# Lending the SBUF of resting weights to the K and V tiles between two layers of a decode kernel

## The chip, the cores and the metric

The kernel runs on one core of a Trainium2 chip. The metric is the device time in microseconds (us). The profiled span, which the profile counts its times from, is some 2 to 3 us shorter than the time. The time of one kernel varies by about 1% from run to run, so single runs are not compared where the difference is small. PE is TensorE, the engine of the matmuls. SyncE (SP in the profile) issues the loads here. PE's granted clock is the share of its full clock that the profile's clock records show.

## The reference

Two identical layers, each an attention block and a gated block, both with a layer norm and a residual. One new token per sequence, four sequences:

```python
B, Sq, D = 4, 1, 512
Hq, Hkv, Sk, Dh = 32, 8, 4096, 128        # four query heads share one K/V head
# attention: q = norm(x) @ wq; softmax(q k^T / sqrt(Dh)) v; @ wo
# gated block: h = sigmoid(norm(x) @ w_gate) * (norm(x) @ w_up); h @ w_down
x = x + A(norm(x)); x = x + B(norm(x))    # layer 1
x = x + A(norm(x)); x = x + B(norm(x))    # layer 2, same weights, same cache
```

Both layers read the same cache: 8 K/V heads ("groups") × 4 sequences × 2 (K and V) tiles of 1 MiB. That is 64 tiles per layer, and almost all of the traffic.

## The kernel before

K and V tiles pass through a ring of eleven SBUF tiles. The weights have fixed places and are loaded once. The second layer visits the groups in reverse, so that the last group of layer 1 (eight tiles) serves as the first of layer 2 without a load. The parts that matter here, with cuts:

```python
NS = 11
ring = [sb(f"ring{i}", [P, T * DH], bf) for i in range(NS)]
wq = sb("wq", [P, KD, H * DH], bf)
wu = sb("wu", [P, KD, F], bf)
wd = sb("wd", [P, 4, 3, D], bf)
wd_r = sb("wd_r", [P, 2, D], bf)
...
def pump():                       # loads, in the fixed order of the queue
    while queue:
        if isinstance(queue[0], tuple):
            if not free:
                return            # a K/V load needs a free tile
            load_kv(*queue.pop(0))
        else:
            queue.pop(0)()        # a weight has its own place

def done_with(n, kind):           # after group n's scores ("k") or values ("v")
    for b in range(B):
        if n == G - 1:
            slots[n + 1, kind, b] = slots[n, kind, b]   # shared by both layers
        else:
            free.append(slots[n, kind, b])
    pump()
```

All loads are issued by SyncE on one queue, in this order. Each waits on the semaphores of whatever last used its tile. In the last two groups of a layer the work is arranged for latency. In layer 2, three of the last group's V tiles go through one set of matmuls (`values(n + 1, (0, 1, 2))`), and the fourth has a path of its own, called "the last tile" here.

## Time and profile before

| | before |
|---|---|
| time, median of 3 | 382.67 us (382.48 to 382.71) |
| profiled span | 380.5 us |
| bytes read | 139.73 MB |
| loads stand still between the layers | about 215 to 225.5 us |
| last V tile landed (issue + time to landing: 355.1 + 11.5) | 366.6 us |
| its matmuls start | 369.18 us |
| w_down's matmuls of layer 2 start | 376.79 us |

These are two rows of the page: the span in 40 slices, with the busy share of the load engines in tenths and the rate they reached.

```profile
DMA  7999999999999999999999539999999999999940
GB/s 307 403 387 400 396 381 413 388 405 405 380 416 387 391 407 390 421 419 371 370 396 397 234 92 375 416 393 411 399 404 404 398 411 391 418 421 387 387 149 2
```

The loads run at about 400 GB/s everywhere except in the first slice, in slices 22 and 23 (counted from 0) and in the last two. So the time is the time of the loads plus two stretches without them. The table by windows shows the first stretch closely. Its columns are the stretch, its length, PE's granted clock, the share of the load engines and GB/s.

```profile
214.00:216.00 2.00, 1.00 0.30 127
216.00:218.00 2.00, 1.00 0.00 0
...
224.00:226.00 2.00, 0.97 0.51 66
226.00:228.00 2.00, 0.88 0.76 311
228.00:230.00 2.00, 0.50 0.88 326
```

Counting every window from 214 to 232 us against 400 GB/s (a window of 2 us at rate r loses 2 × (1 − r/400) us) gives 12.0 us of lost transfer time. The cause is in SyncE's timeline (start, length, what it issued, how many) and in its waits (who waited for whom, total us, times, longest us):

```profile
197.43 27.45 SPq L251 DMA_DIRECT2D ring<-in_A_k_cache_dram  x4
224.92 9.55 SPq L251 DMA_DIRECT2D ring<-in_A_v_cache_dram  x4
```

```profile
SPq L78 <- PE S_ps L437: 48.1, 9, 23.6
```

Four K loads in one row last 27 us because the fourth waited 23.6 us for layer 2's first scores (PE S_ps), the first event that freed a ring tile. Eight tiles were held by the shared group, and three had already been filled again.

The second stretch is the tail. This is PE's timeline there: the values matmuls of three V tiles, the last tile's matmuls (L567), then w_gate's and w_up's (L616), and w_down's (L658). A row gives start, length, line, what was done and how often; a bracket at its end gives the idle time before it and what ended that.

```profile
364.08 3.56 PE L513 MATMUL O_ps<-ring,pt_sb 128*16 128x512 bf16 x24 [2.35 <-issue]
...
369.18 0.62 PE L567 MATMUL S_ps<-ring,pt_sb 128*16 128x128 bf16 x32
...
374.26 0.93 PE L616 MATMUL O_ps<-wu,xT 128*4 128x448 bf16 x16
...
376.79 0.84 PE L658 MATMUL Y_ps<-wd,hT 128*4 128x128 bf16 x48
```

From the last tile's matmuls it takes 5.1 us until w_up is used and 7.6 us until w_down is used. During that time the load engines have nothing to do.

### The profile page before, as it was taken

To read this page: it belongs to the slowest core of one execution; us is meant where nothing else is said; L and a number is where in the kernel's file an instruction comes from. 1 tells how busy PE (TensorE), PEld (TensorE's weight loads), DVE (VectorE), ACT (ScalarE), POOL (GpSimd) and SP (SyncE) were. 2 spreads that over 40 slices of the span, in tenths; PEclk is the share of its full clock that TensorE was granted. 3 is DMA by queue.
4 is the path that set the end of the run, shared out by engine and by line. 5 is a ranking of instruction groups with operands and counts; after the bars stand their busy time and mean duration, and the time that the engine had idled before them with its cause. 6 is when DMAs were issued, how large, how long until landed. Compare 5 with 4: busy or idle time off the path is not lost. (4 is left out here: it accounts for less than half of the span.)

```text
span 380.5 us, 5087 instructions
## 1 busy us (share of the span) xinstructions
PE 179.4 (47%) x2136; PEld 77.6 (20%) x2136; DVE 195.3 (51%) x280; ACT 85.3 (22%) x169; POOL 9.8 (3%) x36
## 2 busy tenths in 40 slices
PE   0336243442454414522359856463444454541876
PEld 0213021121121211211124422121121121211333
DVE  3744733638355383398310348482928384697212
ACT  1113040040220402204210132323232231304311
POOL 6100000000000000000000000000000000000000
PEclk9995565555555555556669976665656566665589
DMA  7999999999999999999999539999999999999940
GB/s 307 403 387 400 396 381 413 388 405 405 380 416 387 391 407 390 421 419 371 370 396 397 234 92 375 416 393 411 399 404 404 398 411 391 418 421 387 387 149 2
DMA packets 48550, 140.06 MB, mean 368 GB/s; under 512 B 2192, under 2 KB 6544, under 8 KB 40848
## 3 DMA queue, kind: packets, MB, share of 16 engines
q1 hardware_dynamic: 48480, 139.73, 95.5%
q8 instruction: 17, 0.28, 0.3%
q14 instruction: 5, 0.04, 0.0%
q10 hardware_dynamic: 48, 0.01, 0.0%
HBM read 139.73 MB, written 0.00 MB: 367 GB/s over the span
## 5 line engine op out<-in xcount | busy, mean ns | idle before, releaser
L428 DVE STREAM_TRANSPOSE ring<-ring 128x2048 int32<-128x2048 int32 x60 | 137.2, 2299 | 40.8 <-DMA ring<-in_A_k_cache_dram 40.0
L454 ACT ACTIVATE p_sb<-S_ps,nbias,rs_q 128x1024 bf16<-128x1024 f32 x16 | 41.9, 2617 | 188.1 <-DVE nbias L450 188.1
L437 PE MATMUL S_ps<-ring,qbd 128*16 128x512 bf16 x512 | 56.5, 616 | 36.7 <-DVE ring L428 36.4
L513 PE MATMUL O_ps<-ring,pt_sb 128*16 128x512 bf16 x496 | 58.2, 605 | 10.9 <-DMA ring<-in_A_v_cache_dram 8.3
L447 DVE TENSOR_REDUCE ml<-S_ps 128x1 f32<-128x1024 f32 x16 | 19.5, 1219 | 51.5 <-PE S_ps L437 51.5
L466 PE MATMUL PT_ps<-sel_p,p_sb 128*128 128x64 bf16 x128 | 9.3, 235 | 62.5 <-ACT p_sb L454 62.5
L589 PE MATMUL Y_ps<-wo,oT 128*4 128x128 bf16 x256 | 7.9, 260 | 51.1 <-DVE oT L540 51.0
L437 PEld LDWEIGHTS S_ps<-ring,qbd 128*16 128x16 bf16 x512 | 15.7, 120 | 67.7 <-issue 42.4
L513 PEld LDWEIGHTS O_ps<-ring,pt_sb 128*16 128x16 bf16 x496 | 17.6, 122 | 40.7 <-issue 37.4
L524 ACT ACTIVATE o_sb<-O_ps,wcol 128x512 f32<-128x512 f32 x16 | 11.0, 687 | 54.3 <-PE O_ps L513 47.9
L466 PEld LDWEIGHTS PT_ps<-sel_p,p_sb 128*128 128x128 bf16 x128 | 7.0, 123 | 75.3 <-ACT p_sb L454 74.4
L476 DVE STREAM_TRANSPOSE tr<-ml 128x64 f32<-128x64 f32 x16 | 3.8, 237 | 28.9 <-ACT p_sb L454 28.9
L531 PE MATMUL M_ps<-ident,o_sb 128*128 128x128 f32 x64 | 13.3, 342 | 10.5 <-ACT o_sb L524 10.5
L589 PEld LDWEIGHTS Y_ps<-wo,oT 128*4 128x4 bf16 x256 | 4.1, 93 | 56.1 <-DVE oT L540 56.1
L416 ACT ACTIVATE qbd<-Q_ps 32x64 bf16<-32x64 f32 x60 | 12.9, 214 | 6.4 <-PE Q_ps L402 5.9
L336 PE MATMUL S_ps<-perm 128*128 128x256 bf16 x78 | 14.1, 288 | 0.0
L531 PEld LDWEIGHTS M_ps<-ident,o_sb 128*128 128x128 f32 x64 | 8.5, 169 | 21.5 <-ACT o_sb L524 20.5
L491 DVE TENSOR_TENSOR el<-ee,tr 128x16 f32<-128x16 f32 x16 | 2.8, 175 | 19.4 <-ACT ee L489 19.4
L471 ACT ACTIVATE pt_sb<-PT_ps 128x512 bf16<-128x512 f32 x16 | 9.5, 596 | 10.6 <-PE PT_ps L466 10.6
L402 PE MATMUL Q_ps<-qT,perm 128*128 128x16 bf16 x64 | 4.4, 179 | 15.7 <-ACT qT L399 15.5
L540 DVE TENSOR_REDUCE oT<-M_ps 128x16 bf16<-128x64 f32 (+1 forms) x16 | 3.1, 197 | 15.5 <-PE M_ps L531 15.5
L381 POOL TENSOR_TENSOR rs_h<-vpe,mhalf 128x1 f32<-128x1 f32 x2 | 1.1, 550 | 353.5 <-DVE vpe L377 200.5
(91 smaller groups left out, 111.5 us busy)
## 6 DMA issues: line engine op xcount, KB each, us to landing
ring<-in_A_k_cache_dram SPq DMA_DIRECT2D x60, 1024.0 KB, 14.1
ring<-in_A_v_cache_dram SPq DMA_DIRECT2D x60, 1024.0 KB, 17.2
wq<-in_A_wq_dram SPq DMA_DIRECT2D x4, 1024.0 KB, 14.2
wo<-in_A_wo_dram SPq DMA_DIRECT2D x4, 1024.0 KB, 14.6
wg<-in_B_w_gate_dram SPq DMA_DIRECT2D x1, 1792.0 KB, 16.3
wu<-in_B_w_up_dram SPq DMA_DIRECT2D x1, 1792.0 KB, 16.8
wd<-in_B_w_down_dram SPq DMA_DIRECT2D x1, 1536.0 KB, 23.7
wd_r<-in_B_w_down_dram SPq DMA_DIRECT2D x2, 128.0 KB, 21.0
```

Of the source, the lines that this page charges most:

```text
L336: fn = lambda e: e.matmul(bank[:, 0:256], lhsT=perm[:, 0, :], rhs=perm[:, 0:2, :].rearrange("p n x -> p (n x)"), start=True, stop=True)
L416: fns.append(lambda e, o=o, i=i: e.activation(o, i, ACTF.Copy))
L428: S.put("dve", lambda e: e.transpose(v, v), reads=[f"r{s}"], writes=[f"r{s}"])
L437: fns.append(lambda e, q=q, nn=nn, b=b, kt=kt: e.matmul(S_ps[32 * b:32 * b + 16, q * 512:(q + 1) * 512], lhsT=qbd[:, qi, b, nn, :], rhs=kt ...
L447: "dve", lambda e: e.tensor_reduce(ml[:, 0:1], S_ps[:], AX.X, ALU.max, negate=True),
L454: lambda e: e.activation(p_sb[:].rearrange("p tb (j q) -> p q tb j", q=4), S_ps[:].rearrange("p (q tb j) -> p q tb j", q=4, tb=8), ACTF.Ex ...
L466: fns.append(lambda e, tb=tb: e.matmul(PT_ps[:, tb * 64:(tb + 1) * 64], lhsT=p_sb[:, tb, :], rhs=sel_p[:], start=True, stop=True,))
L471: "act", lambda e: e.activation(pt[:].rearrange("p t x -> p (t x)"), PT_ps[:], ACTF.Copy),
L513: fns.append(lambda e, tb=tb, b=b, v=v: e.matmul(O_ps[32 * b:32 * b + 16, :], lhsT=pt[:, tb, 16 * b:16 * b + 16], rhs=v[:, :, tb, :], star ...
L524: "act", lambda e: e.activation(o_sb[:], O_ps[:], ACTF.Copy, scale=wc[:, 0:1]),
L531: fns.append(lambda e, a=a: e.transpose(M_ps[:, a * P:(a + 1) * P], o_sb[:, a * P:(a + 1) * P], ident[:]))
L589: fns.append(lambda e, h=h, j=j: e.matmul(Y_ps[32 * j:32 * j + B, 0:P], lhsT=oT[:, g * R + h, :], rhs=wo[:, g * R + h, j * P:(j + 1) * P], ...
```

## The change

Between the layers, w_up, w_down and the last quarter of w_q have just been read. That quarter isn't needed again, once the q projections of layer 2's first two groups are both made at the layer's start. The change gives this space to the ring, as four more tiles. The three tiles in w_up and w_down are used once. The quarter of w_q stays in the ring as a twelfth tile. Three quarters of w_up, and w_down, are loaded again behind the last V tile. In addition, the last group's three values tiles are split into two and one. The core of the diff, with cuts:

```diff
+    ud = sb("ud", [P, KD * F + 14 * D], bf)          # w_up and w_down in one piece
+    XB = KD * F + 14 * D - NX * TS                   # NX = 3 ring tiles at its end
+    ring += [ud[:, XB + i * TS:XB + (i + 1) * TS] for i in range(NX)]
+    ring.append(wq[:, 3].rearrange("p k n -> p (k n)"))
+    shared = {NS: ["wu_b"], NS + 1: ["wu_b", "wd"], NS + 2: ["wd", "wd_r0", "wd_r1"], NS + 3: ["wq3"]}
...
     def put(self, eng, fns, reads=(), writes=(), dma=None, after=()):
+        for k in after:                              # wait for the readers of k alone
+            deps += self.readers.get(k, ())
...
     def done_with(n, kind):
-            else:
+            elif not NS <= slots[n, kind, b] < NS + NX:
                 free.append(slots[n, kind, b])
+    def lend(*extra):
+        free.extend(NS + i for i in extra)
+        pump()
...
+    queue += [lambda: load_wu("wu_b", 1, KD), load_wd]      # the reload, last in the queue
...
+    # after w_up's matmuls of layer 1: lend(0); after w_down's: lend(1, 2)
+    # after both q projections of layer 2's start: free.append(NS + NX); pump()
...
         if last:
-            values(n + 1, (0, 1, 2))
+            values(n + 1, (0, 1))
+            values(n + 1, (2,))
```

## The prediction

> **What bounds the kernel.** The loads. The page's slice rows show the DMA engines at nine tenths in almost every slice, about 400 GB/s; 139.7 MB were read. Two stretches break this. In the table by windows the engines move almost nothing from about 215 to 225.5 us, between the layers: with the ramps on both sides I count 12.0 us of lost transfer time at 400 GB/s. The cause is in SyncE's timeline: eight of eleven K/V tiles hold the group that both layers share, three take the next K tiles, and the next load (224.55) waits for the second layer's first scores (PE S_ps, 23.6 us, the longest entry of the wait view). The second stretch is the tail: the last bytes land near 366.0, the output is issued at 378.24 and the span ends at 380.5.
>
> **What the change does.** It issues four tiles (4.2 MB) inside the gap: one after w_up's matmuls (about 214.7), two after w_down's (217.1), one after both q projections that use the last quarter of w_q (about 220.3). At 2.65 us a tile (the cadence at which the last V tiles of layer one land) the queue then stays fed until scores free four more at about 225. In the gap before, bytes came about 1 us after the issue, so some 1.5 to 2 us are still lost: the gain is about 10.2 us. After it the second layer is still load bound: a group costs 20.6 us of loading, but took 17.1 us from scores to scores (221.05 to 238.13) with its data there. Counting free slots against landed tiles I find no new starvation; the w_q quarter even stays as a twelfth slot.
>
> **What it costs.** w_up's three quarters and w_down, 3.2 MB or about 8 us, go behind the last V tile. The Trainium skill ("DMA: Bandwidth & Descriptors", Queues, rings and completion order) says descriptors on an engine are consumed in ring order; the V tiles landing one by one agree, so the last V tile shouldn't be delayed. The reload hides in the tail: w_up's matmuls start 5.1 us after the last tile's values matmuls, w_down's 7.6 us after. w_up (3.5 us) hides wholly. w_down doesn't quite: while it and its two small remainders landed in layer one, the rate fell to 224 to 333 GB/s for 4 us, 1.2 us lost, so I put it about 9.5 to 9.8 us after the last V tile, an estimate from those windows. Splitting the last values matmuls (two tiles, then the third) lets PE run while the third tile lands: before, all 24 began at 364.08 and delayed the last tile's to 369.18, 3.2 us after landing. Now about 1.2 us. So w_down could be used 8.8 us after the last V tile and waits about 1 us. Tail: about 0.8 us shorter net. The extra q projection (16 matmuls, 0.6 us) replaces one inside group 8; off the path.
>
> **Prediction.** 382.67 - 10.2 - 0.8 = 371.7 us; 80% range 369.4 to 374.8. Faster by over 2%: 0.91, within 2%: 0.08, slower: 0.01.
>
> **What would show it.** DMA windows between 216 and 226 near 400 GB/s instead of none; the last V tile landing about 10 us earlier; DMA busy another 8 to 9 us after it; PE's w_down matmuls waiting for a DMA by 0 to 2 us, w_up's for none; last-tile matmuls about 1 us after landing.
>
> **What would make it wrong.** The lent tiles arriving with gaps between them (one tile in flight at a time); loads starving around 250 to 262 because slots now come free later than loads want them; w_down's reload landing slower than estimated, each us of it one us of time; the last V tile delayed by the reload behind it.

## The result, and the profile after

The changed kernel took 373.07 us (median of 4 runs, 371.18 to 374.07) against 382.58 us (4 runs) for the kernel before. The ratio is 0.9753, with a 95% interval of 0.9709 to 0.9797. Ratios in this document are the mean time of one kernel's runs over that of the other's of the same rounds, so they are not quite the ratios of the medians quoted. Executions over 1.5% slower than the fastest of the same kernel are left out of the means. The result is correct.

| | before | after |
|---|---|---|
| profiled span | 380.5 | 370.1 us |
| bytes read | 139.73 | 142.94 MB |
| last V tile landed | 366.6 | 357.6 us (343.3 + 14.3) |
| its matmuls start, after landing | 2.6 | 0.8 us |
| w_down's matmuls start, after that landing | 10.2 | 8.8 us |

The two rows of the page after:

```profile
DMA  7999999999999999999999999999999999999993
GB/s 306 404 387 396 401 385 400 396 396 414 388 398 399 380 421 384 408 422 415 341 393 391 412 330 384 416 388 421 377 411 400 402 408 396 419 420 386 387 397 104
```

The hole is closed: slice 23 went from 92 to 330 GB/s, and the loads run on almost to the end. These are the windows after, in the gap, then three from a later part of layer 2 that matter below:

```profile
214.00:216.00 2.00, 1.00 0.86 197
216.00:218.00 2.00, 1.00 0.74 307
...
224.00:226.00 2.00, 1.00 1.05 389
226.00:228.00 2.00, 0.79 0.93 336
228.00:230.00 2.00, 0.50 1.03 387
258.00:260.00 2.00, 1.00 0.97 386
260.00:262.00 2.00, 0.82 0.97 337
262.00:264.00 2.00, 0.50 1.02 380
```

By the same count, 1.9 us are lost in the gap now instead of 12.0 us. SyncE's timeline shows the four lent loads, each issued right after the last reader of its space:

```profile
214.52 0.33 SPq L263 DMA_DIRECT2D ud<-in_A_k_cache_dram  x1
217.02 0.93 SPq L263 DMA_DIRECT2D ud<-in_A_v_cache_dram  x2
220.25 0.37 SPq L263 DMA_DIRECT2D wq<-in_A_v_cache_dram  x1
```

In PE's timeline of the tail after the change, the last tile's matmuls are now L611, w_up's L660 and w_down's L704:

```profile
355.01 1.89 PE L557 MATMUL O_ps<-wq,pt_sb 128*16 128x512 bf16 x8 [0.70 <-DMA wq<-in_A_v_cache_dram]
358.45 0.62 PE L611 MATMUL S_ps<-ring,pt_sb 128*16 128x128 bf16 x32
...
363.54 0.93 PE L660 MATMUL O_ps<-ud,xT 128*4 128x448 bf16 x16
366.41 0.95 PE L704 MATMUL Y_ps<-ud,hT 128*4 128x128 bf16 x56 [0.34 <-DMA ud<-in_B_w_down_dram]
```

w_up's matmuls wait for nothing, and w_down's wait 0.34 us for the reload. The spans differ by 10.4 us and the mean times by 9.5 us. The profiled run of the kernel before was a long one: over the 11 runs of it in each later set the mean span was 379.2 to 379.7 us.

### The profile page after: what moved, and what is told of

It is laid out like the page before. It is cut to its first block, busy times and chain, and to the rows that moved or that the text cites. A ratio compares the mean times of both kernels' runs of the same rounds, so it can differ in the third digit from the quotient of the medians.

```text
span 370.1 us, 5088 instructions
## 1 busy us (share of the span) xinstructions
PE 178.4 (48%) x2133; PEld 76.7 (21%) x2133; DVE 195.6 (53%) x281; ACT 84.5 (23%) x168; POOL 9.8 (3%) x36
## 3 DMA queue, kind: packets, MB, share of 16 engines
q1 hardware_dynamic: 49712, 142.94, 100.5%
HBM read 142.94 MB, written 0.00 MB: 386 GB/s over the span
## 5 line engine op out<-in xcount | busy, mean ns | idle before, releaser
L472 DVE STREAM_TRANSPOSE ring<-ring 128x2048 int32<-128x2048 int32 x57 | 130.4, 2299 | 30.0 <-DMA ring<-in_A_k_cache_dram 29.2
L557 PE MATMUL O_ps<-ring,pt_sb 128*16 128x512 bf16 x456 | 56.0, 588 | 10.2 <-DMA ring<-in_A_v_cache_dram 8.4
L575 PE MATMUL M_ps<-ident,o_sb 128*128 128x128 f32 x64 | 13.3, 342 | 10.4 <-ACT o_sb L568 10.4
L361 PE MATMUL S_ps<-perm 128*128 128x256 bf16 x75 | 14.0, 292 | 0.0
L557 PE MATMUL O_ps<-wq,pt_sb 128*16 128x512 bf16 x24 | 9.1, 546 | 0.7 <-DMA wq<-in_A_v_cache_dram 0.7
## 6 DMA issues: line engine op xcount, KB each, us to landing
ring<-in_A_k_cache_dram SPq DMA_DIRECT2D x57, 1024.0 KB, 14.2
wq<-in_A_wq_dram SPq DMA_DIRECT2D x4, 1024.0 KB, 14.2
wq<-in_A_v_cache_dram SPq DMA_DIRECT2D x3, 1024.0 KB, 14.2
```

Of the source, the lines that this page charges most:

```text
L361: fn = lambda e: e.matmul(bank[:, 0:256], lhsT=perm[:, 0, :], rhs=perm[:, 0:2, :].rearrange("p n x -> p (n x)"), start=True, stop=True)
L472: S.put("dve", lambda e: e.transpose(v, v), reads=[f"r{s}"], writes=[f"r{s}"])
L557: fns.append(lambda e, tb=tb, b=b, v=v: e.matmul(O_ps[32 * b:32 * b + 16, :], lhsT=pt[:, tb, 16 * b:16 * b + 16], rhs=v[:, :, tb, :], star ...
L575: fns.append(lambda e, a=a: e.transpose(M_ps[:, a * P:(a + 1) * P], o_sb[:, a * P:(a + 1) * P], ident[:]))
```

## The experiments

My theory was that the loads bind and their lost time adds up; four tiles in the gap bring it back; the reload hides behind the tail; and the split shortens the tail. The rivals were that the rearranged code or the twelfth tile brings the gain, or that the reload costs something after all. Twelve kernels ran in three sets, each set on one chip with 11 runs of the kernel before beside it. "Gain" below is the mean time of the kernel before in the same set less that of the kernel in question.

| kernel | ratio to before | 95% interval | gain |
|---|---|---|---|
| set 1: changed kernel again | 0.9745 | 0.9721 to 0.9769 | 9.6 us |
| set 1: no reload (wrong result) | 0.9731 | 0.9711 to 0.9752 | 10.1 us |
| set 1: nothing lent | 0.9965 | 0.9948 to 0.9983 | 1.2 us |
| set 1: no split | 0.9771 | 0.9743 to 0.9798 | 8.7 us |
| set 2: no twelfth tile | 0.9806 | 0.9777 to 0.9836 | 7.4 us |
| set 2: only w_q's quarter lent | 0.9884 | 0.9856 to 0.9912 | 4.4 us |
| set 2: only w_up's and w_down's space lent | 0.9808 | 0.978 to 0.9836 | 7.3 us |
| set 2: meant as "lent late" (same program, see below) | 0.9754 | 0.972 to 0.9788 | 9.3 us |
| set 3: reload ahead of the last V tiles | 1.0028 | 0.9982 to 1.0074 | -0.9 us |
| set 3: w_down reloaded first | 0.9865 | 0.9824 to 0.9907 | 5.3 us |
| set 3: w_down's wait split | 0.9752 | 0.9717 to 0.9787 | 9.6 us |
| set 3: the same, and w_up before w_gate | 0.9778 | 0.9738 to 0.9818 | 8.7 us |

**The changed kernel again.**

> The changed kernel again, as an anchor for this set. Both theories: about 9.5 us faster than the kernel before in time (ratio 0.975), about 10.4 us shorter in span.

It came out as expected in time (9.6 us). Its profiled run was slow (391.17 us against 371.08 to 373.50 us of the other five) and is used nowhere here.

**Nothing lent, nothing reloaded.** The edit removes the three lendings and the reload. The layout, the early q projection and the split stay.

```diff
-    queue += [lambda: load_wu("wu_b", 1, KD), load_wd]
-            lend(0)
-            lend(1, 2)
-            free.append(NS + NX)
-            pump()
```

> The changed kernel with nothing lent and nothing reloaded: what stays is the w_q layout, the early q projection and the split of the last values matmuls. Theory (the filled gap is worth 9 us, the split about 1.7 us): 1.5 to 2.0 us faster than the kernel before. Rival (the rearranged code itself, not the lending, brings much of the gain): 4 us or more faster than the kernel before.

The gain was 1.2 us, a little under the expectation. The rearranged code isn't where the gain is. Lending, with its reload, is worth 9.6 − 1.2 = 8.4 us in this set. In this run the last tile landed at 354.6 + 11.6 = 366.2 us, and its matmuls began at 367.12, 0.9 us later, instead of 2.6 us later.

**No split.**

```diff
-            values(n + 1, (0, 1))
-            values(n + 1, (2,))
+            values(n + 1, (0, 1, 2))
```

> The changed kernel with the last group's three tiles again in one set of values matmuls. Theory: the last tile's matmuls start 2.6 us after its landing instead of 0.85 us, w_down's wait of 0.34 us goes away, so 1.2 to 1.6 us slower than the changed kernel. Rival (w_down's landing, not PE, ends the tail): no slower than 0.4 us.

It was 1.0 us slower than the changed kernel (9.6 − 8.7, before rounding 0.97), a little under the expectation. The intervals overlap, but the trace shows the mechanism. The last tile landed at 342.6 + 14.3 = 356.9 us, its matmuls began at 359.82, 2.9 us later, and w_down's matmuls waited for no load. So the split is worth about 1 us here; the 1.2 us with nothing lent is of the same size, but there the rearranged code is in it too.

**No reload.** The edit removes the `queue +=` line alone. The second layer then multiplies with K and V data in w_up's and w_down's place, so the result is wrong.

> The changed kernel without the reload of w_up and w_down at the end; its second layer's result is wrong on purpose. Theory (the reload hides behind the tail's computation, only a 0.34 us wait of PE is left): 0.3 to 0.5 us faster than the changed kernel, the last V tile landing at the same time to 0.3 us. Rival (the reload competes with the last V tiles or with the tail, since the last V tile came only 9.0 us earlier rather than the 10.2 us estimated): 1 us or more faster, with the last V tile landing 0.7 us or more earlier.

The gain was 0.5 us more than the changed kernel's, which the times do not resolve (the intervals overlap). The trace does: the last V tile landed at 343.4 + 14.2 = 357.6 us, as with the reload, and w_down's matmuls begin without a wait, 7.6 us after the last tile's instead of 8.0 us:

```profile
358.56 0.62 PE L610 MATMUL S_ps<-ring,pt_sb 128*16 128x128 bf16 x32
...
366.17 0.95 PE L703 MATMUL Y_ps<-ud,hT 128*4 128x128 bf16 x56
```

So 3.2 MB behind the last V tile did not delay it. This is what the Trainium skill's page "DMA: Bandwidth & Descriptors" (Queues, rings and completion order) leads one to expect, as it says that descriptors on one engine are consumed in ring order.

**The reload ahead of the last V tiles.** The same bytes stand four tiles earlier in the queue.

```diff
-    queue += [lambda: load_wu("wu_b", 1, KD), load_wd]
...
     for n, kind in order:
+        if (n, kind) == (NLAYER * G - 1, "v"):
+            queue += [lambda: load_wu("wu_b", 1, KD), load_wd]
         queue += [(n, kind, b) for b in range(B)] + after.get((n, kind), [])
```

> The reload of w_up and w_down stands in the queue before the last group's four V tiles instead of behind them. Theory (loads bind until the last V tile, and bytes ahead of it cost their whole time): the last V tile lands about 8.5 us later, w_down's wait is gone, about 8 us slower than the changed kernel, which leaves about 1.5 us of gain over the kernel before. Rival (the reload is cheap wherever it stands): within 2 us of the changed kernel.

The whole gain is gone (−0.9 us, not distinguishable from none), so the place in the queue is worth 9 to 10 us (the profiled spans, 379.4 and 370.1 us, differ by 9.3 us). The last V tile landed at 348.4 + 17.8 = 366.2 us, 8.6 us later than in the changed kernel, as the theory says. The further loss is PE's: it stood idle for 10.6 us before the last group's values, its granted clock was 0.50 from 358 to 364 us instead of 1.00, and the last tile's matmuls began 1.9 us after landing instead of 0.8 us. These are the row of the first values matmuls, and one of the table by windows (stretch, length, PE busy with its instructions, granted clock, load share, GB/s):

```profile
361.10 3.16 PE L558 MATMUL O_ps<-ring,pt_sb 128*16 128x512 bf16 x14 [10.56 <-DMA ring<-in_A_v_cache_dram]
```

```profile
360.00:362.00 2.00, 0.90 (x6) 0.50 1.06 388
```

**w_down reloaded first.**

```diff
-    queue += [lambda: load_wu("wu_b", 1, KD), load_wd]
+    queue += [load_wd, lambda: load_wu("wu_b", 1, KD)]
```

> The reload turned round: w_down first, then w_up. Theory (w_up's matmuls could start 5.9 us after the last V tile and w_down's 8.4 us after; the whole reload lands 8.7 us after): w_up's matmuls now wait about 2.8 us for their load, 2.3 to 2.8 us slower than the changed kernel. Rival (only the total of the reload counts): the same within 0.5 us.

It gained 5.3 us, some 4 us less than the changed kernel (whose gains in sets 1 and 2 were 9.6 and 9.3 us), where 2.3 to 2.8 us had been expected. The direction was right and the size wrong. PE's timeline here:

```profile
363.55 0.74 PE L660 MATMUL PT_ps<-wg,xT 128*4 128x448 bf16 x12
367.73 1.66 PE L660 MATMUL O_ps<-ud,xT 128*4 128x448 bf16 x16 [3.44 <-DMA ud<-in_B_w_up_dram]
369.33 1.46 PE L361 MATMUL S_ps<-perm 128*128 128x256 bf16 x6
```

w_up waits 3.44 us, a little more than I had estimated. After this wait, the same sixteen matmuls take 1.66 us instead of 0.93 us, and the six filler matmuls after them (L361, whose result nothing reads) 1.46 us instead of 0.83 us, another 1.4 us together. The table by windows (stretch, length, PE busy with its instructions, granted clock, load share, GB/s) names the cause:

```profile
364.00:366.00 2.00, 0.29 (x8) 1.00 0.56 209
366.00:368.00 2.00, 0.27 (x4) 0.84 0.06 23
368.00:370.00 2.00, 2.00 (x20) 0.50 0.00 0
```

The granted clock fell to half just before PE resumed. The Trainium skill's page "TensorE: Matmul & The Clock Gate" (Part 1: The HAM clock gate) states that PE's clock is halved after an idle window of about 3.4 us and comes back after about as long a busy one. The 3.44 us of idle here and the clock of 0.50 after it agree. An idle window is not the only way to the lower clock, though: in the trace of the kernel before, the clock was 1.00 from 219 to 220 us and 0.50 from 221 to 224 us, while PE was busy for 0.64 us or more in every single us from 216 to 224. No run here explains that fall. In this kernel, a load that came late in a chain of matmuls cost its wait (3.44 us), and then a slow stretch (1.4 us).

**Only part of the space lent.** First w_q's quarter alone (without reload), then w_up's and w_down's three tiles alone (with the whole reload):

```diff
 w_q's quarter alone:
-    queue += [lambda: load_wu("wu_b", 1, KD), load_wd]
-            lend(0)
-            lend(1, 2)
 w_up's and w_down's space alone:
-            free.append(NS + NX)
-            pump()
```

> Only the quarter of w_q is lent, and nothing needs to be reloaded; the split stays. Theory (each lent tile whose load starts in the gap gives back its 2.65 us of transfer): about 2.6 us faster than with nothing lent, so 4.2 to 4.7 us faster than the kernel before. Rival (the count of ring tiles, not the gap, matters): the same gain as the changed kernel or none.

> Only w_up's and w_down's three tiles are lent, with the whole reload; the quarter of w_q isn't. Theory: the gap is open again for one tile, 2.3 to 2.7 us slower than the changed kernel. Rival: no slower than 0.5 us, as the fourth tile is lent only 4 us before the scores free four more.

Against the 1.2 us with nothing lent (set 1), w_q's quarter alone gained 3.2 us more. That is at or a little above the 2.65 us of one tile, and no reload had to be paid. The three tiles alone gained 7.3 us, 2.0 us less than the changed kernel of that set. Both speak for the theory: each tile brings back about its transfer time. But in the first of them the quarter also stays in the ring as a twelfth tile, so that run alone doesn't tell the load in the gap from the extra tile. The next run bears on this.

**No twelfth tile.** Here the fourth tile is lent in the gap, but not kept.

```diff
-            elif not NS <= slots[n, kind, b] < NS + NX:
+            elif slots[n, kind, b] < NS:
                 free.append(slots[n, kind, b])
```

> The changed kernel, but the quarter of w_q is lent once and not kept as a twelfth tile of the ring. Theory (the gain is the gap; eleven tiles kept the load engines busy in the second layer before): within 0.5 us of the changed kernel. Rival (the twelfth tile carries part of the gain): 1 us or more slower, with rates under 380 GB/s in stretches of the second layer.

This was a miss, and the most instructive of the runs. It is 1.9 us slower than the changed kernel of the same set (9.3 − 7.4) and as slow as the kernel that doesn't lend the fourth tile at all (7.4 and 7.3 us). In the times, nothing can be seen of lending a tile in the gap and not keeping it; the two intervals leave room for about 1 us. The windows of this kernel show where the loads stand still instead (columns as before):

```profile
224.00:226.00 2.00, 1.00 1.05 388
226.00:228.00 2.00, 0.53 1.05 389
...
258.00:260.00 2.00, 1.00 0.82 262
260.00:262.00 2.00, 0.56 1.09 338
262.00:264.00 2.00, 0.50 0.81 266
```

The kernel that lends only w_up's and w_down's space shows in the same windows:

```profile
224.00:226.00 2.00, 1.00 0.36 100
226.00:228.00 2.00, 0.77 0.96 307
...
258.00:260.00 2.00, 1.00 1.03 401
260.00:262.00 2.00, 0.81 0.97 389
262.00:264.00 2.00, 0.50 0.77 263
```

Without the fourth tile, the loads lose 2.0 us at the end of the gap (224 to 228). With it, but not kept, nearly nothing there (0.1 us), but 1.8 us from 256 to 266. There the loads wait again, this time for layer 2's third scores. SyncE's timelines, counted issue by issue, agree: up to those scores (257 to 258 us) both kernels had issued 19 tiles of layer 2, and the changed kernel 20. It had issued two K tiles at 250.86 and 251.23, one of them into w_q's quarter, where the kernel without the twelfth tile could issue only one, at 249.72. The changed kernel loses 0.3 us from 256 to 266.

The sizes are less sure than the direction. The kernel with only w_up's and w_down's space lent loses 0.9 us from 256 to 266 as well, and seven other traces, of kernels that lend and keep the same four tiles, lose nothing in five cases and about 1.0 us in two (without the reload, and with w_down's wait split). At the end of the layer, the first load of the reload is issued at 345.98 us in the changed kernel (345.2 to 346.8 us in six traces of kernels that keep the tile and reload last), at 347.67 us without the twelfth tile and at 348.55 us with the fourth tile never lent. So by these single traces the load in the gap is worth about 0.9 us, and keeping the tile 0.9 to 2.4 us: probably the larger part of the fourth tile's worth lies in its staying.

**Meant as "lent late".** I moved all four lendings in the program to the place where w_q's quarter is lent.

```diff
-            lend(0)
-            lend(1, 2)
-            free.append(NS + NX)
+            free.extend(NS + i for i in range(NX + 1))
```

> The same four tiles and the same reload, but all four lent only at the point where the quarter of w_q is (about 220.25 us instead of 214.5 and 217.0). Theory (what counts is transfer time not lost): the loads restart 5.7 us later, so 5 to 6 us slower than the changed kernel. Rival (what counts is how many tiles are held ahead): no slower than 1 us.

This experiment didn't do what it was meant to. SyncE issued the loads at 214.64, 217.13 and 220.36 us, as before. An issue waits for the semaphores of its space's readers, and these don't depend on where the program text puts the lending. As SyncE's order didn't change either, this is the changed kernel once more, and it serves as the anchor of set 2 (9.3 us). What a later restart of the loads costs was not measured by itself.

**Two attempts at a better version.** The first lets w_down's first 48 matmuls wait for the main part of the reload alone. The second adds to that w_up's matmuls before w_gate's in layer 1, so that the first tile is lent earlier.

```diff
-        S.put("pe", fns, reads=["hT", "wd", "wd_r0", "wd_r1"], writes=["Y"])
+        S.put("pe", fns[:48], reads=["hT", "wd"], writes=["Y"])
+        S.put("pe", fns[48:], reads=["hT", "wd_r0", "wd_r1"], writes=["Y"])
 and in the second:
-        for w, keys, bank, bkey in ((wg, ...), (wu, ...)):
+        mats = ((wg, ...), (wu, ...))
+        for w, keys, bank, bkey in (mats if last else mats[::-1]):
```

> The changed kernel, with w_down's first 48 matmuls waiting for its main part alone and only the last 8 for the two small remainders. Theory: the 0.34 us wait of PE goes away or moves behind the 48, so 0.1 to 0.3 us faster, which times alone may not resolve; the span from the last V tile's matmuls to the output shortens. Rival (the main part lands last): no change.

> As the one before, and in the first layer w_up's matmuls run before w_gate's, so its first tile is lent about 0.7 us earlier. Theory: the loads restart 0.7 us earlier, but the chain to the scores is about 0.5 us later, which opens the gap's end again: 0 to 0.6 us faster than the one before. Rival: slower, if the later release of the four tiles costs more than the earlier start gives.

The first gained 9.6 us, the same as the changed kernel within the noise. In its trace w_down's matmuls begin 7.6 us after the last tile's (366.81 and 359.19), so the wait of 0.34 us is gone, as expected. The second gained 8.7 us. Its first tile was issued at 213.84 instead of 214.52, but the next two at 217.57 instead of 217.02, and no gain is to be seen. Neither is shown to be better than the changed kernel.

## Why the prediction was right

The predicted 371.7 us (range 369.4 to 374.8) met 373.07 us at first, and 371.08 to 373.50 us in five later fast runs. Its parts, point by point:

- **The loads bind, and the gap between the layers is the thing to fill.** Right. With nothing lent, 1.2 us of the gain remain. One tile alone brought 3.2 us more. With the same bytes put ahead of the last V tiles, the whole gain is gone.
- **"The gain is about 10.2 us."** Right in mechanism and somewhat too large. In the gap, 10.1 us came back by the windows (12.0 to 1.9 us lost). But 0.3 us were lost anew from 256 to 266 us, and the last V tile landed 9.0 us earlier. Over the runs, lending without the cost of the reload is worth 8.9 us (10.1 − 1.2). The windows leave about 0.8 us between 9.8 and 9.0 unexplained, which a single pair of traces can't settle.
- **"I find no new starvation; the w_q quarter even stays as a twelfth slot."** Nearly right for the kernel as it was built, but the argument for it was incomplete. I had counted the moments at which tiles come free and treated the twelfth tile as an extra. Without it, the loads starve for 1.8 us by the third group, and the kernel is 1.9 us slower. With it, 0.3 us are left. That the tile was in the change was good fortune as far as this step goes; what was plainly wrong is the expectation of the run without it.
- **The last V tile isn't delayed by the reload.** Right. It landed at 357.6 us with and without the reload.
- **"I put it about 9.5 to 9.8 us after the last V tile."** Too pessimistic. The reload was complete 8.7 us after it (352.2 + 14.1 = 366.3 us), 3.2 MB at 369 GB/s on average. I had carried over the slow windows of layer 1 (224 to 333 GB/s) in full.
- **w_down waits about 1 us.** It waited 0.34 us, because the reload was complete earlier.
- **The split lets PE start the last tile's matmuls 1.2 us after landing instead of 3.2 us.** They began 0.8 us after it instead of 2.6 us (the 3.2 us count from the last bytes near 366.0 us, the 2.6 us from the landing at 366.6 us). Over the runs, the split is worth 1.0 to 1.2 us.
- **The tail is 0.8 us shorter net.** In the traces 1.4 us (10.2 to 8.8 us from landing to w_down), and over the runs about 0.7 us (split 1.2, reload −0.5, the latter not resolved by the times).

The sum was 11.0 us, and the runs gave 9.3 to 9.6 us. What was over-estimated was the gap's term, by about 1 us. In the pair of traces the tail's term erred the other way (1.4 us for 0.8 us), so that the sum came closer to the measurement than its largest term did, which is luck.

## What to carry to other kernels

Where loads bind, look for the stretches in which they stand still, ask which buffer they wait for, and lend them space that happens to rest. Here a reload was nearly free (0.5 us by the means, which the times don't resolve) when it stood behind the last load that computation waits for and was ordered by first use. In the wrong order it cost some 4 us, and in front of that load its full transfer time, and PE's clock besides. A tile lent in the gap and then taken away lost much of its worth when the ring next ran out; count the tiles issued up to each later release before crediting it.

## What the Trainium skill lacked or had wrong

- "HBM Reference" (Specifications) gives about 358 GB/s per core in its table and about 425 GB/s for a core that streams alone in the text below. Here, with one core of the program at work, 10 us windows in layer 2 held 377 to 422 GB/s. The page says that the smaller figure is a core's share when both cores of a pair stream, so nothing here shows it wrong; used for this case, it would have made every transfer estimate too long.
- "DMA: Bandwidth & Descriptors" (Specifications) puts the smallest transfer for line rate at 512 B. While w_down with its runs of 3 KB and 1 KB landed in layer 1, at full engine share, the rate was 224 to 333 GB/s, and the reload as a whole ran at 369 GB/s, against 377 to 422 GB/s in the 10 us windows of K and V in 2 and 8 KB runs. No run here isolates the cause (w_down's two remainders are also small loads, 128 KB each), so this doesn't show the page wrong.
- "TensorE: Matmul & The Clock Gate" (Part 1) agrees with one stretch: after 3.44 us of idle, the clock was 0.50, and sixteen matmuls took 1.66 us instead of 0.93 us. Its idle window doesn't account for the fall from 1.00 to 0.50 at about 221 us of the kernel before, where PE was busy for at least 0.64 us of every us.
